# Attention, maxout and PReLU layers on one core: the last batch's gate stage, with its row splits, factor loads and weight loads put in another order

## The chip, the cores and the metric

The kernel runs on one core of one Trainium2 chip. The metric is the device time of one execution in microseconds (us), lower is better. Before the change it is 775.16 us, the median of three runs (775.11 to 776.03).

## What is computed

```python
def reference(q, k, v, ...):                      # 4 batches, 8 heads, 576 positions, 64 wide
    scores = q @ k.T / sqrt(64)                   # masked: 4 heads local, 4 heads strided
    x = softmax(scores) @ v                       # -> x: 2304 tokens x 512
    h = maximum(maximum(x @ w1, x @ w2), x @ w3)  # 512 -> 768, "gates"
    x2 = h @ w_out                                # 768 -> 512
    y = x2 @ w_in                                 # 512 -> 2048
    g = maximum(y, 0) + alpha * minimum(y, 0)
    return g @ w_out2                             # 2048 -> 512
```

All of it is in float32. The kernel splits each operand of a product into a high and a low part and makes three matmuls of them (high x high, high x low, low x high).

## The kernel before, in words

The program has two halves. In the first (to 413 us of the span), batches 0 to 2 go through attention, the three gate layers and the first output layer ("out1"), in an order made by a planner (`Weave`); the weights of the second layer pair are prepared meanwhile. The last batch's gates and out1 are written out by hand, as a generator, `last_net`. In the second half, three blocks of 768 tokens (each in two column halves of 384) go through the last two layers.

The change is in `last_net` and in the loop that drives it (`for n, _ in enumerate(last_net(B - 1))`). `last_net` yields after each unit of work, and the loop puts other work between units; n is the number of the unit.

- Units 0 to 11 (`GATES_LAST`) are ordinary gate products, 12 matmuls of 288 columns each (L570). Meanwhile eight factors of the tokens, "T1" to "T4", are made: `make(m)` splits them in high (ACT) and low (DVE).
- Units 12 to 53 are six groups of seven products (k = 3 to 8). A product is six matmuls into one of eight PSUM banks (L735). Seven products by Winograd's scheme give four quarters of one gate matrix times the tokens. Of each group ACT copies the first product out of its bank (L752), and DVE adds the six others up in a chain that starts from that copy (`add`, L722). A group belongs to g = 0, 1 or 2. With g = 1 and 2 DVE also takes the running maximum (`greatest`), and with g = 2 the finished h is split: ACT casts its high part, DVE makes its low part (L205, L208 in `split`). One factor pair ("ws", two tiles of 512 KB) is loaded for each group into the pool `hw` of eight tiles (`load_factors`).
- Units 54 to 61 are out1: eight products of 18 matmuls (L592), each copied out by ACT (L784) and stored to DRAM as x2.

Into these units the loop weaves the splitting of the second block's rows (block 1), which batches 1 and 2 have left in DRAM. For each of its two halves SP loads four row tiles ("xs", `early_load`), POOL makes four sums (`early_sums`, L805), and then seven `early_split`s follow, one every second unit: ACT casts the high part into a tile of pool `xst`, POOL makes the low part (L208), and one unit later SP stores the tile to DRAM ("xd<-xst", `early_store`, L829). The pool `xst` has two tiles, so a cast waits until the store of two splits earlier has landed. The loop also loads the nine first tiles of output weights ("w<-wo", `load_ow`, L855), one every four units from unit 12 on. Each engine works its instructions off in the order in which they are written, and SP issues all of the loads and stores in one queue.

Of the kernel before, what the change touches and what calls it, by code (L numbers as in the profile page):

```python
# [10 lines left out]
F32 = mybir.dt.float32  # L11
# [3 lines left out]
ALU = mybir.AluOpType  # L15
# [25 lines left out]
NOW = 9  # L41
NG = 3 * NF1 // 2
NP = 3
X_SPLIT = 13


class Weave:
# [112 lines left out]
def attention_maxout_prelu_kernel(  # L160
# [13 lines left out]
    nc = tc.nc  # L174
# [28 lines left out]
    def split(hi, lo, src, hi_engine, lo_engine):  # L203
        if hi_engine is nc.scalar:
            hi_engine.copy(hi, src)  # L205
        else:
            hi_engine.tensor_copy(hi, src)
        lo_engine.tensor_tensor(out=lo, in0=src, in1=hi.bitcast(F32), op=ALU.subtract)  # L208
# [5 lines left out]
    def pool(stack, name, bufs, side="left"):  # L214
        return stack.enter_context(tc.tile_pool(name=name, bufs=bufs, side=side, reuse_waits="tile"))
# [25 lines left out]
    def bank():  # L241
        return ps.tile([P, 512], F32, tag="bank", name="bank")
# [370 lines left out]
    GATES_LAST = [(hf, f) for f in range(2 * NP // 3) for hf in range(2)]  # L613
# [60 lines left out]
    def last_net(b):  # L674

        factors, st = {}, {}

        def load_factors(k):
            if k < NG:
                for i in range(2):  # L680
                    t = words["s", k, i] = hw.tile([P, 2, DM], F32R, tag="w", name="w")
                    nc.sync.dma_start(t.bitcast(F32), sd[k - NP][i][:, :, :])
            else:
                n, i = divmod(k - NG, 2)
                load_h(n, ((0, 2), (1, 3))[i])

        for k in range(NP, NP + 4):
            load_factors(k)
        rows = [[p_.tile([P, 2, HB], F32, tag=tag, name=tag) for _ in range(2)]
                for p_, tag in ((xsp, "xs"), (xst, "xst"))]  # L690
        for i in range(2):
            for r in range(2):
                for h in range(2):
                    x = xt[b, i + 2 * r, h].bitcast(F32)
                    nc.vector.tensor_tensor(out=rows[i][r][:, h, :HALF], in0=x[:, 0], in1=x[:, 1], op=ALU.add)
        named = []
        for i in range(2):
            b11, b12, b21, b22 = (t[:, h, :HALF] for t in rows[i] for h in range(2))
            t2, t3, t4 = (temp() for _ in range(3))
            for out_, x, y in ((t3, b22, b12), (b12, b12, b11), (t2, b22, b12), (t4, b21, t2)):  # L700
                nc.vector.tensor_tensor(out=out_, in0=x, in1=y, op=ALU.subtract)
            named += [("T1", i, b12), ("T2", i, t2), ("T3", i, t3), ("T4", i, t4)]
            for c, (name, h) in enumerate((("11", 0), ("21", 0), ("22", 1))):
                factors[name, i] = xt[b, i + 2 * (c > 0), h]
        named.sort(key=lambda it: it[0])

        def make(m):
            name, i, x = named[m]
            t = factors[name, i] = (xt[b, i, 1] if name == "T4" else
                                    (xp if m < 3 else tf).tile([P, 2, HALF], F32R, tag="x", name="x"))  # L710
            split(t[:, 0], t[:, 1], x, nc.scalar, nc.vector)

        for n, (hf, f, g) in enumerate(units(GATES_LAST)):
            gate_unit(b, hf, f, g, st)
            if n < 6:
                make(n)
            yield
        for m in range(6, 8):
            make(m)

        def add(out_, bank, other, op=ALU.add):
            nc.vector.tensor_tensor(out=out_, in0=bank, in1=other, op=op)  # L722

        for k in range(NP, NG):
            p, g = divmod(k, 3)
            w0, w1_ = (words["gate", 2 * p + j, g] for j in range(2))
            sa, sb = (words["s", k, i] for i in range(2))
            new = kept_temp if g == 0 else temp

            def product(w, off, name):  # L730
                bank_ = bank()[:, :HALF]
                m = 0
                for c in range(2):
                    for wi, xi in PAIRS:
                        nc.tensor.matmul(bank_, w[:, wi, off + c * P:off + (c + 1) * P],  # L735
                                         factors[name, c][:, xi, :], start=m == 0, stop=m == 5)
                        m += 1
                return bank_

            def greatest(hf, j, c):  # L740
                if g == 0:
                    st[hf, j] = c
                    return
                t = st[hf, j]
                add(t, t, c, ALU.max)
                if g == 2:
                    h = st["h", hf, 2 * p + j] = hp.tile([P, 2, HALF], F32R, tag="x", name="h")
                    split(h[:, 0], h[:, 1], t, nc.scalar, nc.vector)

            x = product(w0, 0, "11")  # L750
            u = new()
            nc.scalar.copy(u, x)  # L752
            yield
            x = product(sb, 256, "T2")
            v = new()
            add(v, x, u)
            yield
            x = product(w0, 256, "21")
            add(u, x, u)
            greatest(0, 0, u)  # L760
            yield
            x = product(sb, 0, "T3")
            w = new()
            add(w, x, v)
            yield
            x = product(w1_, 256, "T4")
            c21 = new()
            add(c21, x, w)
            greatest(0, 1, c21)
            yield  # L770
            x = product(sa, 0, "T1")
            add(w, x, w)
            add(v, x, v)
            greatest(1, 1, w)
            yield
            x = product(sa, 256, "22")
            load_factors(k + 4)
            add(v, x, v)
            greatest(1, 0, v)
            yield  # L780
        for hf in range(2):
            for dc in range(NCC):
                xo = tp.tile([P, HALF], F32, tag="t", name="xo")
                nc.scalar.copy(xo, out1_products(b, hf, dc, st))  # L784
                store_x2(b, hf, dc, xo)
                yield
# [23 lines left out]
    def split_x2(blk, k, i, pool, tag, lo_engine=nc.vector):  # L810

        t = pool.tile([P, 2, HB], F32R, tag=tag, name=tag)
        split(t[:, 0], t[:, 1], xs.pop((blk, PRODUCTS[k][1], i)), nc.scalar, lo_engine)
        return t

    early_rows, early_parts = {}, []

    def early_load(blk, i, pool, tag):
        early_rows[blk, i] = load_x2(blk, i, pool, tag)
# [1 line left out]
    def early_sums(blk, i):  # L821
        sum_x2(blk, i, early_rows.pop((blk, i)), nc.gpsimd)

    def early_split(blk, i, k):
        early_parts.append((blk, k, i, split_x2(blk, k, i, xst, "xst", nc.gpsimd)))

    def early_store():
        for blk, k, i, t in early_parts:
# [31 lines left out]
    for b in range(B):  # L860
        first, last = (-32, -8) if b == 0 else ((b - 1) * NUNITS + (16 if b == 1 else 3), b * NUNITS - 3)
# [24 lines left out]
    tsp = pool(ctx, "tsp", 3, "right")  # L886
    xst = pool(ctx, "xst", 2, "right")
    sx = ExitStack()
    tq = pool(sx, "tq", 8, "right")
    tf = pool(sx, "tf", 3, "right")  # L890

    def temp():
        return tq.tile([P, HALF], F32, tag="t", name="t")
# [1 line left out]
    def kept_temp():  # L895
        return tp.tile([P, HALF], F32, tag="t", name="t")

    ready = {X_SPLIT + 19 * half + 2 * k: (1, half, k) for half in range(2) for k in range(7)}
    first, gates = 3 * len(GATES_LAST), 3 * len(GATES_LAST) + 7 * (NG - NP)
    fetched = [first + 4 * i for i in range(9)]  # L900
    for n, _ in enumerate(last_net(B - 1)):
        if n in fetched:
            load_ow()
        if n - 1 in ready:
            early_store()
        for half in range(2):
            if n == X_SPLIT + 19 * half - 5 + 2 * half:
                early_load(1, half, xsp, "xs")
            if n == X_SPLIT + 19 * half - 1:
                early_sums(1, half)  # L910
        if n in ready:
            early_split(*ready[n])
        if n == gates - 5:
            rows = [load_x2(0, 0, xsp, "xs"), load_x2(0, 1, xst, "xst")]
        if n == gates - 1:
            sx.close()
            x0x.close()
            xmp = pool(ctx, "xmp", 1, "right")
        if n == gates:
            sum_x2(0, 0, rows[0], nc.vector)  # L920
        if n == gates + 1:
            sum_x2(0, 1, rows[1], nc.vector)
        for i, ks in {0: [(0, range(7))], 2: [(1, range(4))], 3: [(1, range(4, 7))]}.get(n - gates, []):
            for k in ks:
                x2h[0, k, i] = split_x2(0, k, i, xmp, f"x{k}{i}")
# [258 lines left out]
    for n in range(NQ * NBLK):  # L1184
        blk, q = divmod(n, NQ)
# [75 lines left out]
```

## Time and profile before

| | |
|---|---|
| median of three runs | 775.16 us |
| the profiled execution's own time | 777.17 us |
| its span, first to last instruction | 775.4 us |
| PE busy | 743.9 us, 96% of the span |
| DVE, ACT, POOL busy | 628.7, 466.0, 50.4 us |
| mean granted TensorE clock | 0.982 |
| matmuls of the gate groups (L735) | 252, 38.3 us busy, 9.1 us of idle time before them |

The page also cuts the span into 40 slices of 19.4 us. PE stands at 9 tenths in nearly all of them; apart from the start three neighbouring slices, the 19th to 21st, from about 349 to 407 us, are at 7, and in the last two of them the clock row stands at 8 tenths. The stretch of the last batch is there. Where rows below name a tile, "bank", "ph" and "po" are PSUM banks, "t" the temporary tiles, "xst" the split rows and "xd" their place in DRAM.

### The profile page before, as it was taken

Reading aid. Unit: us, or ns where it says so; the run is one execution under the profiler, and the core shown is the slowest. Engines: PE = TensorE matmul, PEld = TensorE weight load, DVE = VectorE, ACT = ScalarE, POOL = GpSimd, SP = SyncE. Lnnn points to the kernel's source line nnn. Section 1 sums busy time; section 2 is a strip of 40 time slices with the busy share of each in tenths; the row PEclk is TensorE's granted clock in tenths of the full one; section 3 lists DMA queues with packets and bytes.
Section 4 is the critical chain, followed back from the end, with each engine's and each line's share of the span. In section 5 each row is a group of like instructions: output and inputs, shape, how many; then the busy total and the mean of one; then the engine's idle time right before and its main releaser. Section 6 shows DMA issues by size and latency. Waiting matters only on the chain.

```text
span 775.4 us, 16198 instructions
## 1 busy us (share of the span) xinstructions
PE 743.9 (96%) x5668; PEld 724.1 (93%) x5668; DVE 628.7 (81%) x1663; ACT 466.0 (60%) x1252; POOL 50.4 (6%) x60
## 2 busy tenths in 40 slices
PE   5799999999999999997779999999999999999998
PEld 4699999999999999997779999999999999999997
DVE  4899998998998998555476988886988896888885
ACT  5987889568676896222135656654566554465571
POOL 1000000000000000032400211000211000000000
PEclk9789999999999999999889999999999999999999
DMA  6467769995999775669775889999888999877362
GB/s 239 144 222 238 225 209 328 354 358 204 331 334 337 259 252 213 240 244 339 247 268 174 265 266 315 353 400 376 299 316 289 344 403 375 278 253 251 122 186 87
DMA packets 88929, 211.97 MB, mean 273 GB/s; under 512 B 11024, under 2 KB 41232, under 8 KB 88848
## 3 DMA queue, kind: packets, MB, share of 16 engines
q1 hardware_dynamic: 88848, 210.94, 78.4%
q8 instruction: 45, 0.74, 0.4%
q14 instruction: 36, 0.29, 0.1%
HBM read 154.80 MB, written 56.10 MB: 272 GB/s over the span
## 4 chain that ended last, share of the span: by engine, by line
PE 80%; DMA 8%; DVE 5%; ACT 2%; POOL 2%; issue 1%; SPq 1%; DVEq 0%; ACTq 0%; POOLq 0%
PE ph L1122 21%; PE bank L570 21%; PE po L954 18%; PE bank L592 9%; PE ph L954 3%; DMA xd<-xst 3%; PE bank L311 3%; PE bank L382 3%; PE bank L357 2%; DMA w<-ws 1%; POOL xst L208 1%; DMA xs<-x 1%; DMA w<-wo 1%; DMA wo<-w 1%; DVE e L319 1%
## 5 line engine op out<-in xcount | busy, mean ns | idle before, releaser
L1122 PE MATMUL ph<-x,w 128*128 128x384 f32 x990 | 199.9, 337 | 0.6 <-ACT c L1132 0.5
L570 PE MATMUL bank<-x,w 128*128 128x288 f32 x1440 | 197.9, 297 | 0.0
L570 PEld LDWEIGHTS bank<-x,w 128*128 128x128 f32 x1440 | 192.5, 189 | 1.9 <-issue 0.2
L954 PE MATMUL po<-w,g 128*128 128x256 f32 x1296 | 181.1, 281 | 0.0
L954 PEld LDWEIGHTS po<-w,g 128*128 128x128 f32 x1296 | 174.9, 189 | 0.3
L1122 PEld LDWEIGHTS ph<-x,w 128*128 128x128 f32 x990 | 165.2, 188 | 1.0 <-ACT c L1132 0.7
L1128 DVE TENSOR_TENSOR c<-ph,c 128x384 f32<-128x384 f32 x165 | 89.2, 553 | 39.2 <-PE ph L1122 38.2
L947 ACT CAST g<-c 128x384 fp32r<-128x384 f32 x96 | 48.6, 506 | 90.4 <-DVE c L1106 48.9
L592 PE MATMUL bank<-h,w 128*128 128x288 f32 x576 | 82.5, 302 | 5.0 <-ACT h L205 4.9
L592 PEld LDWEIGHTS bank<-h,w 128*128 128x128 f32 x576 | 79.0, 193 | 7.0 <-ACT h L205 5.5
L326 ACT ACTIVATE e<-e,nm 96x128 f32<-96x128 f32 (+2 forms) x176 | 68.0, 395 | 7.6 <-DVE nm L319 7.6
L250 ACT CAST w<-word 128x512 fp32r<-128x512 f32 x100 | 57.5, 587 | 22.6 <-DMA wh<-w 8.4
L253 DVE TENSOR_TENSOR w<-word,w 128x512 fp32r<-128x512 f32 x100 | 62.8, 641 | 9.4 <-ACT w L250 9.1
L1072 ACT ACTIVATE c<-c 128x384 f32<-128x384 f32 x96 | 50.5, 526 | 32.2 <-DVE c L1128 30.9
L1076 DVE SCALAR_TENSOR_TENSOR c<-c 128x384 f32<-128x384 f32 x96 | 54.7, 570 | 8.7 <-ACT c L1073 8.7
L1073 ACT ACTIVATE c<-c,nalpha 128x384 f32<-128x384 f32 x96 | 59.2, 617 | 3.1
L948 DVE TENSOR_TENSOR g<-c,g 128x384 fp32r<-128x384 f32 x96 | 55.1, 573 | 1.9 <-ACT g L947 1.9
L441 ACT ACTIVATE word<-raw 128x512 f32<-128x512 f32 x56 | 37.5, 676 | 18.3 <-DMA raw<-in_w 14.7
L735 PE MATMUL bank<-x,w 128*128 128x288 f32 x252 | 38.3, 313 | 9.1 <-ACT t L752 6.9
L735 PEld LDWEIGHTS bank<-x,w 128*128 128x128 f32 x252 | 36.5, 203 | 10.8 <-ACT t L752 7.6
L948 DVE TENSOR_TENSOR g<-k,g 128x384 fp32r<-128x384 f32 x72 | 36.9, 550 | 8.0 <-ACT g L947 8.0
L1106 DVE TENSOR_TENSOR k<-c 128x384 f32<-128x384 f32 x72 | 40.3, 587 | 0.0
(93 smaller groups left out, 834.0 us busy)
## 6 DMA issues: line engine op xcount, KB each, us to landing
w<-wh SPq DMA_DIRECT2D x72, 512.0 KB, 5.5
raw<-in_w SPq DMA_DIRECT2D x50, 512.0 KB, 4.7
w<-wo SPq DMA_DIRECT2D x48, 512.0 KB, 6.1
w<-wp SPq DMA_DIRECT2D x36, 512.0 KB, 7.0
wh<-w SPq DMA_DIRECT2D x24, 512.0 KB, 5.1
xd<-xst SPq DMA_DIRECT2D x28, 384.0 KB, 6.0
x<-xd SPq DMA_DIRECT2D x28, 384.0 KB, 8.4
ws<-w SPq DMA_DIRECT2D x12, 512.0 KB, 3.9
```

The source lines that it names most:

```text
L250: (nc.scalar.copy if e == "ACT" else nc.vector.tensor_copy)(out_, in_)
L253: nc.vector.tensor_tensor(out=out_, in0=x, in1=y, op=ALU.subtract)
L326: nc.scalar.activation(tl[ek][:nq, j, i, :nk], tl[ek][:nq, j, i, :nk], AF.Exp, bias=tl["nm", u][:nq, j, i:i + 1], scale=-1.0, accum_out=tl ...
L570: nc.tensor.matmul(acc, words["gate", f, g][:, wi, cc * P:(cc + 1) * P], xt[b, cc, hf][:, xi, :], start=n == 0, stop=n == 3 * NCC - 1)
L592: nc.tensor.matmul(acc, words["mix", f][:, wi, dc * P:(dc + 1) * P], st["h", hf, f][:, xi, :], start=n == 0, stop=n == 3 * NF1 - 1)
L735: nc.tensor.matmul(bank_, w[:, wi, off + c * P:off + (c + 1) * P], factors[name, c][:, xi, :], start=m == 0, stop=m == 5)
L948: return g, lambda: nc.vector.tensor_tensor(out=g[:, 1], in0=x, in1=g[:, 0].bitcast(F32), op=ALU.subtract)
L954: nc.tensor.matmul(bank[:, NH * half:NH * (half + 1)], g[:, gi, t * P:(t + 1) * P], w[:, wi, off:off + NH], start=first and i == 0, stop=l ...
L1073: nc.scalar.activation(a, a, AF.Copy, scale=nalpha[:, f:f + 1])
L1076: nc.vector.scalar_tensor_tensor(out=a, in0=h, scalar=0.0, in1=a, op0=ALU.max, op1=ALU.add)
L1122: nc.tensor.matmul(bank, words["h", n, i][:, wi, off + c * P:off + (c + 1) * P], x2h[blk, k, c][:, xi, :], start=m == 0, stop=m == 5)
L1128: nc.vector.tensor_tensor(out=out_, in0=bank, in1=other, op=ALU.add)
```

## The change

- `X_SPLIT` goes from 13 to 10: the first half's splits stand three units earlier. The second half's stay at units 32 to 44 (10 + 22 instead of 13 + 19).
- `early_load` of the two halves moves from units 8 and 29 to 2 and 23, `early_sums` from 12 and 31 to 8 and 30.
- A second pool of two tiles, `xsu`, takes every other split, so a cast waits for the store of four splits earlier. To make room `tq`, which holds the temporaries, goes from eight tiles to six.
- The first four factor pairs are no longer loaded in one go, but one at the start and the others after units 3, 5 and 7, with the row loads between the first two.
- The nine loads of output weights move from units 12 to 44 to units 53 to 61, behind the gates.
- The low part of an h is recorded in a list and issued by `make_lows` after the matmuls of the next product.

```diff
-X_SPLIT = 13
+X_SPLIT = 10
...
-        for k in range(NP, NP + 4):
-            load_factors(k)
+        load_factors(NP)
...
             if n < 6:
                 make(n)
+            if n in (3, 5, 7):
+                load_factors(NP + n // 2)
             yield
...
+        lows = []
+
+        def make_lows():
+            while lows:
+                h, t = lows.pop(0)
+                nc.vector.tensor_tensor(out=h[:, 1], in0=t, in1=h[:, 0].bitcast(F32), op=ALU.subtract)
...
+                make_lows()
                 return bank_
...
-                    split(h[:, 0], h[:, 1], t, nc.scalar, nc.vector)
+                    nc.scalar.copy(h[:, 0], t)
+                    lows.append((h, t))
...
+            if k == NG - 1:
+                make_lows()
             yield
...
-    def early_split(blk, i, k):
-        early_parts.append((blk, k, i, split_x2(blk, k, i, xst, "xst", nc.gpsimd)))
+    def early_split(blk, i, k, pool=None):
+        early_parts.append((blk, k, i, split_x2(blk, k, i, pool or xst, "xst", nc.gpsimd)))
...
-    tq = pool(sx, "tq", 8, "right")
+    tq = pool(sx, "tq", 6, "right")
     tf = pool(sx, "tf", 3, "right")
+    xsu = pool(sx, "xsu", 2, "right")
...
-    ready = {X_SPLIT + 19 * half + 2 * k: (1, half, k) for half in range(2) for k in range(7)}
-    first, gates = 3 * len(GATES_LAST), 3 * len(GATES_LAST) + 7 * (NG - NP)
-    fetched = [first + 4 * i for i in range(9)]
+    ready = {X_SPLIT + 22 * half + 2 * k: (1, half, k) for half in range(2) for k in range(7)}
+    gates = 3 * len(GATES_LAST) + 7 * (NG - NP)
+    fetched = [gates - 1 + i for i in range(9)]
...
-            if n == X_SPLIT + 19 * half - 5 + 2 * half:
+            if n == X_SPLIT + 21 * half - 8:
                 early_load(1, half, xsp, "xs")
-            if n == X_SPLIT + 19 * half - 1:
+            if n == X_SPLIT + 22 * half - 2:
                 early_sums(1, half)
         if n in ready:
-            early_split(*ready[n])
+            early_split(*ready[n], (xst, xsu)[n // 2 % 2])
```

The order on SP from the second half's row loads to its fourth store, before. "xs<-x" are the row loads, "wh" the first tiles of the next layer's weights, "wo" the output weights, "ws" the factors, "xd_k_h" the store of split k of half h:

```order
L829 DMA xd_6_0_133<-xst 128x768
L855 DMA w<-wo_0_109 128x1024
L797 DMA xs<-x_2_69 128x384
L797 DMA xs<-x_3_70 128x384
L843 DMA w<-wh_0_73 128x1024
L843 DMA w<-wh_2_75 128x1024
L855 DMA w<-wo_1_110 128x1024
L829 DMA xd_0_1_122<-xst 128x768
L829 DMA xd_1_1_124<-xst 128x768
L855 DMA w<-wo_0_111 128x1024
L829 DMA xd_2_1_126<-xst 128x768
```

And with the change:

```order
L841 DMA xd_6_0_133<-xst 128x768
L809 DMA xs<-x_2_69 128x384
L809 DMA xs<-x_3_70 128x384
L682 DMA w<-ws_0_159 128x1024
L682 DMA w<-ws_1_160 128x1024
L855 DMA w<-wh_0_73 128x1024
L855 DMA w<-wh_2_75 128x1024
L841 DMA xd_0_1_122<-xst 128x768
L841 DMA xd_1_1_124<-xst 128x768
L841 DMA xd_2_1_126<-xst 128x768
```

(The four row loads stand as two pairs of such lines.) The output weights are gone from between the stores, and the row loads now stand ahead of the last factor pair.

On ACT, the casts of the first half's splits and the copies that start a group, as the difference of the two programs stands there: before,

```order
L752 COPY t<-bank 128x288
L205 CAST xst<-xs 128x384
L205 CAST xst<-t 128x384
L205 CAST xst<-xs 128x384
L752 COPY t<-bank 128x288
L205 CAST xst<-t 128x384
L205 CAST xst<-xs 128x384
L205 CAST xst<-t 128x384
L205 CAST xst<-xs 128x384
L752 COPY t<-bank 128x288
```

and with the change (ahead of these rows one cast stands before the last gate units' cast of h):

```order
L762 COPY t<-bank 128x288
L205 CAST xst<-t 128x384
L205 CAST xst<-xs 128x384
L205 CAST xst<-t 128x384
L205 CAST xst<-xs 128x384
L762 COPY t<-bank 128x288
L205 CAST xst<-t 128x384
L205 CAST xst<-xs 128x384
L762 COPY t<-bank 128x288
```

Four casts stood ahead of the third group's copy, and now two do. In the second half ACT's order is the same in both programs.

On DVE, the first low parts of the last group (g = 2): before,

```order
L722 TENSOR_TENSOR t<-bank,t 128x288 x2
L722 TENSOR_TENSOR t<-t 128x288
L208 TENSOR_TENSOR h<-t,h 128x288
L722 TENSOR_TENSOR t<-bank,t 128x288 x2
L722 TENSOR_TENSOR t<-t 128x288
L208 TENSOR_TENSOR h<-t,h 128x288
```

and with the change:

```order
L723 TENSOR_TENSOR t<-bank,t 128x288 x2
L723 TENSOR_TENSOR t<-t 128x288
L730 TENSOR_TENSOR h<-t,h 128x288
L723 TENSOR_TENSOR t<-bank,t 128x288 x2
L723 TENSOR_TENSOR t<-t 128x288
L730 TENSOR_TENSOR h<-t,h 128x288
```

Only the line numbers differ: each low part (`h<-t,h`) still stands right behind its maximum (`t<-t`).

## Rows read from the trace of the kernel before

**Rows 1.** Busy time by stretch: width, engines' busy us, granted clock, DMA share, GB/s.

```profile
319.50:338.50 19.00, 19.00 (x146) 19.00 (x145) 9.59 (x23) 5.30 (x14) 1.37 (x2) 1.00 0.79 300
338.50:374.00 35.50, 30.62 (x218) 28.93 (x216) 21.05 (x44) 8.54 (x20) 15.54 (x16) 1.00 0.72 263
374.00:396.00 22.00, 12.85 (x59) 11.84 (x60) 10.00 (x23) 4.45 (x10) 5.64 (x6) 0.73 0.85 282
396.00:413.00 17.00, 17.00 (x123) 17.00 (x123) 12.68 (x27) 8.61 (x22) 0.00 (x0) 0.94 0.59 200
```

**Rows 2.** Timeline of PE: start, length, line, matmuls, idle time before and what ended it.

```profile
305.14 14.55 PE L592 MATMUL bank<-h,w 128*128 128x288 f32 x108
...
338.56 3.91 PE L735 MATMUL bank<-x,w 128*128 128x288 f32 x28
343.00 14.15 PE L735 MATMUL bank<-x,w 128*128 128x288 f32 x104 [0.52 <-DVE x L208]
...
378.23 7.77 PE L735 MATMUL bank<-x,w 128*128 128x288 f32 x36 [4.58 <-ACT t L752]
...
391.49 1.34 PE L592 MATMUL bank<-h,w 128*128 128x288 f32 x3 [3.88 <-ACT h L205]
...
413.04 2.24 PE L1122 MATMUL ph<-x,w 128*128 128x384 f32 x12
```

**Rows 3.** Waits, 330 to 410 us: who waited for whom, us, times, longest.

```profile
ACT xst L205 <- DMA xd<-xst: 27.1, 10, 5.0
```

**Rows 4.** Timeline of ACT around the last group's start.

```profile
380.98 0.52 ACT L205 CAST xst<-xs 128x384 fp32r<-128x384 f32 x1 [2.80 <-DMA xd<-xst]
386.46 0.51 ACT L205 CAST xst<-t 128x384 fp32r<-128x384 f32 x1 [4.96 <-DMA xd<-xst]
...
389.04 0.39 ACT L752 COPY t<-bank 128x288 f32<-128x288 f32 x1
```

**Rows 5.** Landing times, from the views of the stores (first) and of the row loads.

```profile
DMA to landing us min/median/max: 2.3/3.9/6.7
DMA to landing us min/median/max: 5.7/7.2/9.9
```

**Rows 6.** Timeline of POOL: one low part, and the second half's first sum.

```profile
357.62 1.01 POOL L208 TENSOR_TENSOR xst<-xs,xst 128x384 fp32r<-128x384 f32 x1 [1.67 <-ACT xst L205]
368.44 1.02 POOL L805 TENSOR_TENSOR t<-xs 128x384 f32<-128x384 f32 x1 [9.80 <-DMA xs<-x]
```

**Rows 7.** Timeline of DVE: two factors, then groups with g = 0, 2 and 1.

```profile
340.49 2.45 DVE L208 TENSOR_TENSOR x<-t,x 128x288 fp32r<-128x288 f32 x2
342.87 3.42 DVE L722 TENSOR_TENSOR t<-bank,t 128x288 f32<-128x288 f32 x7
...
349.64 0.89 DVE L722 TENSOR_TENSOR t<-t 128x288 f32<-128x288 f32 x1
...
357.88 1.02 DVE L722 TENSOR_TENSOR t<-bank,t 128x288 f32<-128x288 f32 x2 [5.39 <-ACT t L752]
...
362.27 0.46 DVE L208 TENSOR_TENSOR h<-t,h 128x288 fp32r<-128x288 f32 x1 [0.50 <-ACT h L205]
...
366.15 0.46 DVE L208 TENSOR_TENSOR h<-t,h 128x288 fp32r<-128x288 f32 x1 [0.50 <-ACT h L205]
...
378.21 1.02 DVE L722 TENSOR_TENSOR t<-bank,t 128x288 f32<-128x288 f32 x2 [7.01 <-ACT t L752]
...
383.30 0.46 DVE L722 TENSOR_TENSOR t<-t 128x288 f32<-128x288 f32 x1
```

**Rows 8.** Timeline of DVE: block 0's rows, from the first sum to the last low part.

```profile
399.07 0.56 DVE L805 TENSOR_TENSOR t<-xs 128x384 f32<-128x384 f32 x1 [0.89 <-DMA xs<-x]
...
409.78 0.55 DVE L208 TENSOR_TENSOR x<-xst,x 128x384 fp32r<-128x384 f32 x1
```

**Rows 9.** Timeline of SP: issues of the second half's row loads.

```profile
359.52 3.12 SPq L797 DMA_DIRECT2D xs<-x  x4
```

**Rows 10.** Timeline of PE: the first matmuls that use output weights.

```profile
421.36 0.51 PE L954 MATMUL po<-w,g 128*128 128x256 f32 x3
```

## The prediction

> **What bounds the kernel now.** I read the slices of the page first: PE is full except in the last batch's stretch. The view by stretch makes that exact [rows 1]: PE is busy without a gap until 338.5 us, then idle for 35.50 - 30.62 = 4.9 us up to 374 and for 22.00 - 12.85 = 9.2 us up to 396, and full again after that. The granted clock, 1.00 before, is 0.73 in the second of these stretches, a mix of the two levels (1.2 and 2.4 GHz) that follows PE's idle time.
>
> What would the stage take without that? PE's timeline [rows 2] gives undisturbed rates: 104 gate matmuls in 14.15 us are 0.136 us each, 108 out1 matmuls in 14.55 us are 0.1347 each. So 252 gate matmuls need 34.3 us and 144 out1 matmuls 19.4, together 53.7. They take from 338.56 to 413.04, where the next layer's first product begins: 74.5 us. There are **20.8 us** to be had, 14.0 of them idle time and the rest matmuls at a lower clock (36 in 7.77 us are 0.216 each).
>
> Who holds PE? The same timeline names ACT's copy of a group's first product before the largest gap (4.58 us), and ACT's cast of h before the next (3.88). On ACT these two are late because of the split casts written ahead of them: ACT waited 27.1 us in ten waits for stores of split rows [rows 3]. The clearest place is the last group [rows 4]: casts start at 380.98, 386.46 and just before 389.04, each after a wait for a store, and only then runs the copy, 0.39 us long. PE had been some seven products ahead, filled all eight banks, and stopped. A store takes 2.3 to 6.7 us to land [rows 5], and with two tiles every cast waits for the store of two splits earlier. A second cause is the row loads of the second half: POOL's first sum waited 9.80 us for them [rows 6], and everything behind it shifted.
>
> **The change, part by part.**
>
> *Four tiles.* A cast waits for the store of four splits earlier. A round trip is the cast (0.51), POOL's low part (1.01 [rows 6]), some 0.5 for hand-overs and issue, and the store: 5.9 us at the median landing, 8.7 at the longest. Per split that is 1.5 and 2.2 us instead of 3.0 and 4.4. Splits are written one per two products, 1.63 us. So the median store now just keeps up, and a group holds at most four casts.
>
> *First half.* Its loads and sums move ahead by six and four units, its splits by three, and no weights stand between its stores. The first cast runs ahead of the last h cast of the gate units, at about 336; three follow the first group's copy at about 340.5 without a store to wait for; the fifth needs the first store (issued about 338). POOL ends its seventh low part near 348.5. The second and third copies, due at about 345.5 and 351, are not held. Gain: the waits ahead of them go.
>
> *Second half.* Its casts keep their units (32 to 44); only loads, sums and tiles differ. The loads can be issued when the first half's seventh low part is done, 348.5, and take 3.12 us to issue [rows 9]. With landings of 7.2 us (median) they are there by 356 to 358. Four sums at 1.02 bring POOL to 361.5, and low parts follow every 1.0 us. The first store then lands at about 362.5 + 0.3 + 3.9 = 366.7, so the fifth, sixth and seventh casts run at about 367, 368 and 369, and the last group's copy at 369.3. The product that it copies is ready at 338.56 + 0.5 + 35 products of 0.817 + 0.8 = 368.5. It is 0.8 us late, and PE has seven more banks, 5.7 us: no stop. With the longest landings (9.9 and 6.7 us) it is 6.3 us late; that is a rival.
>
> *DVE, which is next in line.* A group with g = 0 takes it 3.42 us, with g = 1 5.55 (378.21 to 383.76), with g = 2 8.73 (357.88 to 366.61) [rows 7]. Six groups are 35.4 us against PE's 34.3: it nearly keeps pace. From the end of the first group's adds (346.3) the others end at 351.9, 360.6, 364.1, 369.6 and 378.3. PE leaves the last group at about 373.4, and no bank is asked for before it is read. out1's first product asks for the second h's low part after 16 of its matmuls, at 375.5; DVE has it 4.85 us into the group (362.27 + 0.46 - 357.88), at 374.5. So there is about 1 us to spare, and I charge 0.3 us, between 0 and the 4 us of the rival below.
>
> *Low parts a product later: nothing.* DVE's order of instructions is the same before and after. The low part still stands directly behind the maximum, so the 0.50 us that it waits for ACT's cast [rows 7] stays, four times in each group with g = 2. They are in the 8.73.
>
> *Temporaries 8 to 6.* Each tile is asked for again only after six others; what it held was last read a group earlier on DVE itself. Cost 0; it is hidden by DVE's own order.
>
> *Factors in turn.* The second pair is now behind the rows on SP, but is needed only at the second group, at 345; SP issued eight such loads in 4 us, and the DMA share is 0.79 there [rows 1]. Cost 0.
>
> *The factor T4.* PE waited 0.52 us for it [rows 2], as DVE took 2.45 us for two splits while POOL was summing [rows 7]. POOL's sums are now earlier but its low parts are there; I leave the 0.5 us in.
>
> *Weights behind the gates.* Nine loads of 512 KB move from the stage to out1. First use is 8.3 us after 413.04 [rows 2, 10], so at about 401 now, and the first of them is issued at about 373. Block 0's rows stand ahead of them. DVE needs 11.3 us for these rows [rows 8]; from 378.3 it ends at 389.6, and PE is ready at 393. Cost 0.
>
> **Sum.** 20.8 - 0.5 - 0.3 = 20.0 us. The profiled execution took 777.17, so it would take 757.2; the median is 2.0 us below the profiled one, and 20.0 off 775.16 gives **755.2**.
>
> **Rivals.**
>
> *The casts still wait* (0.12). If the row loads or stores land as late as the slowest seen, the last group's copy is 6.3 us late. The second h's low part then comes at about 374.8 + 0.4 + 4.85 = 380 for a demand at 375.5: 4.5 us lost, 759.7; if PE's clock falls over it (36 matmuls at 0.216 instead of 0.136), 2.9 more, 762.6. For it: the second half's casts have not moved. Against: less is moved in the stage.
>
> *DVE takes over, through POOL* (0.08). Operations with two tiles in SBUF are slow beside POOL: 2.45 us for two instead of 0.92, 0.89 for a maximum instead of 0.46 [rows 7], while adds out of a bank stay at 0.46. Such losses come to some 3 us in the stage, and the sum keeps them. Twice as many put DVE's end at 381 and PE some 2.5 us back: 757.7. If each of POOL's 22 operations held up one of the 26 such DVE operations for its whole 1.0 us, DVE would be 22 - 3 = 19 us later and nothing gained: 774. The Trainium skill, "SBUF — State Buffer", section "SBUF: two separate sides", states that the two engines share one pair of ports as an exclusive lock, so that the loser blocks for the whole instruction; by that rule packing POOL's work closer works against this change, by between 0 and those 19 us. The trace agrees with the rule's direction (0.89 instead of 0.46), and no run here shows yet how often they meet.
>
> *The weights come too late, and it is slower* (0.03). In out1 SP must now move nine weight tiles, block 0's rows (1.57 MB), two more tiles of 0.79 MB and x2 (1.18 MB), 8.3 MB in all, from 373. At 282 GB/s that is 29 us, to 402; at the 200 of the last stretch [rows 1] 41 us, to 414. If the output products had to wait for all nine, the first would lose 13 us at 200 GB/s (768), and below 170 GB/s, 49 us, more than 20: slower than before. At 160 it would be 779. Against: only the first tile is needed first, and the stretches with loads waiting moved 263 to 300.
>
> *No difference* (0.02): what ends the waits is something that the trace does not name.
>
> **How the numbers follow.** The forecast (0.75) reaches from 753.0 (nothing left over, and half a us for the runs' spread) to 757.5. The range takes in DVE's near case and the first of the late landings: 753.0 to 760.0; outside are the deeper cases of the three rivals, about 0.13. What a measurement of this kernel can tell from no change is about 0.2%, 1.6 us. Faster by more than that are the forecast and nearly all of the first two rivals: 0.94. Within it are the "no difference" case and DVE's far end: 0.03. Slower: 0.03.
>
> **What would show it.** Right: the 252 gate matmuls end at about 373 and the next layer's first product begins at 392.5 to 393.5; the granted clock stays near 1.00 in between; ACT's waits for stores fall from 27.1 to under 8 us; PE names ACT's copy for under 1 us; the low parts' waits of 0.50 are still there. Wrong: a gap on PE of over 2 us with ACT's copy behind it (the casts), DVE's groups longer than 3.4, 5.6 and 8.7 us with PE waiting for banks (POOL), or PE waiting for a weight load after 400.

## The result, and the profile after

The changed kernel takes 755.45 us (median of five runs, 753.71 to 757.36), the kernel before beside it 775.68 us (five runs, 775.11 to 777.19). The ratio is 0.9737, with a 95% interval of 0.9715 to 0.976: 20.2 us faster, where 20.0 were forecast.

The profiled execution took 753.71 us, with a span of 751.9. The view by stretch of the changed kernel (width, busy us of PE, PEld, DVE, ACT and POOL, granted clock, DMA share, GB/s) answers to [rows 1]:

```profile
338.50:374.00 35.50, 34.42 (x256) 33.98 (x255) 28.28 (x61) 8.74 (x21) 15.84 (x16) 1.00 0.89 319
374.00:392.00 18.00, 18.00 (x132) 18.00 (x131) 12.68 (x27) 9.49 (x24) 0.00 (x0) 1.00 0.93 306
```

Idle time of PE falls from 14.0 to 1.1 us, and the clock stays at its upper level. The DMA engines, which were busy for 0.72 and 0.85 of the time and moved 263 and 282 GB/s, now are for 0.89 and 0.93 and move 319 and 306. PE's timeline, beside [rows 2]:

```profile
334.54 33.77 PE L743 MATMUL bank<-x,w 128*128 128x288 f32 x252
368.15 2.18 PE L592 MATMUL bank<-h,w 128*128 128x288 f32 x15
371.31 17.71 PE L592 MATMUL bank<-h,w 128*128 128x288 f32 x129 [0.99 <-ACT h L757]
388.87 2.27 PE L1135 MATMUL ph<-x,w 128*128 128x384 f32 x12
```

All 252 gate matmuls run as one piece, and one gap of 0.99 us is left in out1. In the following, "the stage" is the time from the first gate group's matmul to the next layer's first product, read off such rows. It was 413.04 - 338.56 = 74.5 us and is now 388.87 - 334.54 = 54.3.

The waits in the changed kernel, beside [rows 3] (who waited for whom, us, times, longest):

```profile
ACT xst L205 <- DMA xd<-xst: 4.1, 3, 2.8
DVE h L730 <- ACT h L757: 4.0, 8, 0.5
```

ACT's waits for stores fall from 27.1 to 4.1 us. The eight waits of 0.50 us of DVE's low parts are all there. ACT's timeline in the second half, beside [rows 4]:

```profile
358.71 0.40 ACT L762 COPY t<-bank 128x288 f32<-128x288 f32 x1
361.88 0.51 ACT L205 CAST xst<-xs 128x384 fp32r<-128x384 f32 x1 [2.77 <-DMA xd<-xst]
362.87 0.52 ACT L205 CAST xst<-t 128x384 fp32r<-128x384 f32 x1 [0.47 <-DMA xd<-xst]
364.20 0.52 ACT L205 CAST xst<-xs 128x384 fp32r<-128x384 f32 x1 [0.82 <-DMA xd<-xst]
364.62 0.39 ACT L762 COPY t<-bank 128x288 f32<-128x288 f32 x1
```

The casts still wait, but for 4.1 us in all, and the last group's copy runs 30.1 us into the stage instead of 50.5.

The spans differ by 23.5 us, not 20.2. Of that the stage gives 20.15. It also begins 4.0 us earlier, and what follows it is 0.7 us longer (363.0 instead of 362.4). The earlier start is not the change's doing: the last batch's first gate unit already starts at 315.50 instead of 319.52, and in the kernel with casts on POOL below, which is the kernel before up to that unit, it starts at 316.00. The last section comes back to this.

### The profile page after: what moved, and what is told of

Same layout as the page of the kernel before. It is cut to its first block, busy times and chain, and to the rows that moved or that the text cites. A ratio compares the mean times of both kernels' runs of the same rounds, so it can differ in the third digit from the quotient of the medians.

```text
span 751.9 us, 16191 instructions
## 1 busy us (share of the span) xinstructions
PE 732.7 (97%) x5668; PEld 715.3 (95%) x5668; DVE 630.8 (84%) x1663; ACT 464.4 (62%) x1252; POOL 50.2 (7%) x60
## 4 chain that ended last, share of the span: by engine, by line
PE 91%; DVE 5%; ACT 3%; issue 1%; DMA 0%; DVEq 0%; SPq 0%; ACTq 0%
PE bank L570 26%; PE ph L1135 22%; PE po L967 19%; PE bank L592 10%; PE ph L967 3%; PE bank L311 3%; PE bank L382 3%; PE bank L357 2%; PE bank L743 2%; DVE t L723 2%; ACT e L326 1%; DVE g L961 1%; DVE e L319 0%; DMA k<-in_kTs 0%; DVE k L1119 0%
## 5 line engine op out<-in xcount | busy, mean ns | idle before, releaser
L570 PE MATMUL bank<-x,w 128*128 128x288 f32 x1440 | 197.2, 296 | 0.0
L570 PEld LDWEIGHTS bank<-x,w 128*128 128x128 f32 x1440 | 191.8, 188 | 1.8
L592 PE MATMUL bank<-h,w 128*128 128x288 f32 x576 | 79.9, 297 | 1.1 <-ACT h L757 1.0
L592 PEld LDWEIGHTS bank<-h,w 128*128 128x128 f32 x576 | 77.0, 188 | 2.4 <-ACT h L757 1.2
L250 ACT CAST w<-word 128x512 fp32r<-128x512 f32 x100 | 57.4, 588 | 28.4 <-DMA wh<-w 8.8
L1085 ACT ACTIVATE c<-c 128x384 f32<-128x384 f32 x96 | 50.5, 526 | 32.4 <-DVE c L1141 31.0
L447 DVE SCALAR_TENSOR_TENSOR word<-raw,word 128x512 uint32<-128x512 uint32 x56 | 38.8, 693 | 1.9
L960 ACT CAST g<-k 128x384 fp32r<-128x384 f32 x72 | 33.4, 514 | 7.9 <-PE ph L967 4.0
```

What stands on the lines that cost most here:

```text
L250: (nc.scalar.copy if e == "ACT" else nc.vector.tensor_copy)(out_, in_)
L570: nc.tensor.matmul(acc, words["gate", f, g][:, wi, cc * P:(cc + 1) * P], xt[b, cc, hf][:, xi, :], start=n == 0, stop=n == 3 * NCC - 1)
L592: nc.tensor.matmul(acc, words["mix", f][:, wi, dc * P:(dc + 1) * P], st["h", hf, f][:, xi, :], start=n == 0, stop=n == 3 * NF1 - 1)
L960: nc.scalar.copy(g[:, 0], x)
```

## The experiments

The change has three parts that can stand alone: **tiles** (four tiles, six temporaries), **weights** (output weights behind the gates) and **rows** (order of row loads, factors and first splits). The first four kernels take them one at a time, or leave the tiles out. Each was profiled, and timed beside the kernel before. That took 777.29 us beside these four and 777.23 beside the next ones, some 2 us more than the 775.16 from which my expectations start, so a miss of 2 us in a time says little; the ratio and the stage say more. The six temporaries always come with the four tiles: no run takes them alone.

**Tiles alone.**

```diff
-    tq = pool(sx, "tq", 8, "right")
+    tq = pool(sx, "tq", 6, "right")
+    xsu = pool(sx, "xsu", 2, "right")
...
-            early_split(*ready[n])
+            early_split(*ready[n], (xst, xsu)[ready[n][2] % 2])
```

> The kernel before with one part of the change alone: four tiles for the split rows (and six temporaries instead of eight). Theory A (ACT stands still because a cast waits for the store of two splits earlier; the number of tiles is the cause): the first half's casts run free, the second half's still start late, since its row loads stay at unit 29 with weights in front of them (rows there at about 362 instead of 354, the last group's copy some 6 us late, 4 to 5 us lost on PE). So 760 us, between 758 and 763; ACT's waits for stores fall from 27 to under 12 us. Theory B (the order of the transfers is the cause: row loads come late and 512 KB weight loads stand between the stores; tiles matter little): 768 or more.

Measured: 767.57 us, ratio 0.9892 (0.9864 to 0.9921); stage 402.95 - 336.59 = 66.4 us. That fits neither theory: ACT's waits fell to 13.0 us in five, near what theory A asked for, yet the gain was 8 us instead of 15. The landing times of the stores of split rows, in the kernel with tiles alone, point to the reason:

```profile
DMA to landing us min/median/max: 2.3/7.7/9.5
```

They landed after 7.7 us at the median, against 3.9 before [rows 5]. With four tiles the stores follow each other faster, and the 512 KB loads between them are still there. PE still stopped for 3.20 us behind the copy and for 2.23 and 1.35 us in out1. The table below, where each part is there and is not, bears the reading out.

**Weights alone, rows alone, and both without tiles** (the last is the changed kernel with all splits in one pool).

```diff
-    fetched = [first + 4 * i for i in range(9)]
+    fetched = [gates - 1 + i for i in range(9)]
```

> The kernel before with the nine output weight loads moved behind the gates, and nothing else. Theory A: stores land sooner (about 3 us instead of 3.9), but with two tiles a pair of casts still takes a round trip of about 5 us against 3.3 us of products, so ACT's waits stay above 15 us: 765 to 770. Theory B: the stores and row loads are the cause, so most of the gain is here: 762 or less.

```diff
-X_SPLIT = 13
+X_SPLIT = 10
...
-        for k in range(NP, NP + 4):
-            load_factors(k)
+        load_factors(NP)
...
+            if n in (3, 5, 7):
+                load_factors(NP + n // 2)
...
-            if n == X_SPLIT + 19 * half - 5 + 2 * half:
+            if n == X_SPLIT + 21 * half - 8:
...
-            if n == X_SPLIT + 19 * half - 1:
+            if n == X_SPLIT + 22 * half - 2:
```

> The kernel before with the loads in another order and the first half's splits three units earlier (rows ahead of the later factors, second half's rows six units earlier), with two tiles and the weights in their old place. Theory A: two tiles and weights between the stores keep ACT waiting, more than 18 us: 766 to 771. Theory B: 762 or less.

```diff
-            early_split(*ready[n], (xst, xsu)[n // 2 % 2])
+            early_split(*ready[n])
```

> The changed kernel with all splits in the two tiles of the first pool again; all else as changed. Theory A: casts wait for the store of two splits earlier again; in the second half the copies of the last two groups are each some 8 us late, of which PE's banks hide 5.7: 8 to 10 us lost, 763 to 766. Theory B: 758 or less.

Measured: weights 771.51 us, ratio 0.9919 (0.9888 to 0.995), stage 409.52 - 338.65 = 70.9; rows 772.31 us, ratio 0.9958 (0.9937 to 0.9979), stage 409.53 - 336.39 = 73.1; both 767.66 us, ratio 0.9894 (0.986 to 0.9927), stage 402.67 - 336.24 = 66.4. ACT waited 24.9, 28.6 and 20.8 us for stores. Theory B is out: without the four tiles nothing comes near 762. Theory A had the direction. By the ratios the gains are 6.3, 3.3 and 8.2 us, where it put at least 5.2, 4.2 and 9.2 (and at least 12.2 for tiles alone, which gave 8.4): weights alone did a little better than its least, the three others worse. This led to a new theory C, that the causes need each other.

**Two parts at a time.** Tiles and weights is the kernel before with the two edits above; tiles and rows is the changed kernel with the weights back:

```diff
-    fetched = [gates - 1 + i for i in range(9)]
+    fetched = [first + 4 * i for i in range(9)]
```

> The kernel before with four tiles and with the output weights behind the gates, but the row loads, factors and first splits in their old order. New theory C (two causes that need each other: four tiles let casts go on only if no weight loads stand between the stores; with them the stores land after 7.7 us instead of 3.9, as the kernel with tiles alone showed): most of the 20 us is here; the rows of the second half come some 4 us later than in the changed kernel, which the banks hide: the stage from the first gate group's product to the next layer's first is 55 to 58 us (54.3 in the changed kernel, 74.5 before, 66.4 with tiles alone), the time 755 to 759. If the order of rows and factors is the missing part instead: stage over 61 us, time over 762.

> The changed kernel with the nine output weight loads back in the gate units. Theory C: the stores wait behind weight loads again (landing about 7 us at the median), so ACT's waits for stores rise from 4 us to 10 or more and the stage from 54.3 to 60 to 65 us: 760 to 766. If the order of rows and factors is what tiles alone lacked: stage under 57 us, under 758.

Measured: tiles and weights 761.87 us, ratio 0.9799 (0.9784 to 0.9814), stage 396.86 - 339.12 = 57.7; tiles and rows 761.1 us, ratio 0.979 (0.9773 to 0.9806), stage 395.58 - 336.51 = 59.1. The stage of the first lies where theory C put it, at its upper end, the time 3 us above, of which 2 are the slower kernel before. The second came out 1 us better on the stage than expected, and within the range on the time (by the ratio 1 us better there too); ACT waited 7.4 us for stores, not 10 or more. With that all eight combinations have a trace. The last two columns count from the start of the stage: the start of POOL's first sum of the second half's rows, and the end of POOL's low part in the last split. For that the lines of the kernel before and of the changed kernel are:

```profile
389.21 0.99 POOL L208 TENSOR_TENSOR xst<-xs,xst 128x384 fp32r<-128x384 f32 x1 [1.17 <-ACT xst L205]
```

```profile
364.80 1.02 POOL L208 TENSOR_TENSOR xst<-xs,xst 128x384 fp32r<-128x384 f32 x1 [0.28 <-ACT xst L205]
```

| parts | stage, us | stores land, median us | ACT waits for stores, us | second half's sums begin, us | last split done, us |
|---|---|---|---|---|---|
| none | 74.5 | 3.9 | 27.1 | 29.9 | 51.6 |
| rows | 73.1 | 2.9 | 28.6 | 26.3 | 49.6 |
| weights | 70.9 | 3.2 | 24.9 | 27.6 | 47.1 |
| weights, rows | 66.4 | 2.7 | 20.8 | 23.2 | 42.6 |
| tiles | 66.4 | 7.7 | 13.0 | 28.7 | 42.7 |
| tiles, weights | 57.7 | 4.5 | 4.6 | 22.8 | 35.0 |
| tiles, rows | 59.1 | 6.4 | 7.4 | 21.1 | 36.1 |
| all (the change) | 54.3 | 4.4 | 4.1 | 19.3 | 31.3 |

The gains of the single parts, 1.3, 3.6 and 8.1 us, add up to 13.1; together they give 20.2. Each part is worth most behind the other two: the tiles 12.1 us (66.4 to 54.3), the weights 4.8 and the rows 3.4. The last column goes with the stage: in all eight kernels the stage ends 22.8 to 23.9 us after the last split is done. The third column shows one way in which the parts meet: more tiles let more stores out at once, which costs landing time (3.9 to 7.7), and taking the weights away gives it back (7.7 to 4.5).

**Is ACT's queue the way by which late stores stop PE?** Here the casts of the second block's splits go to POOL, in the kernel before, with its two tiles and its order of loads.

```diff
-        early_parts.append((blk, k, i, split_x2(blk, k, i, xst, "xst", nc.gpsimd)))
+        early_parts.append((blk, k, i, split_x2(blk, k, i, xst, "xst", nc.gpsimd,
+                                                nc.gpsimd if blk == 1 else nc.scalar)))
```

> The kernel before with the second block's split casts on POOL instead of ACT (POOL does cast and low part of each split); tiles, loads and weights as before. If ACT's queue is the way by which late stores stop PE: ACT never waits for a store, the gate groups and out1 run with no gap over 0.6 us (252 gate matmuls in about 34.5 us, out1 in 19 to 20), although the stores still take as long. The chain of splits itself does not get shorter, rather longer (two POOL operations of about 1 us for each, two tiles), so it comes out elsewhere: block 0's rows wait for the last splits, and PE stands before the next layer's first product, 8 to 18 us. Stage 62 to 72 us, time 763 to 772. If PE was held by the transfers or by DVE and not by ACT's queue: gaps of several us remain inside the gate groups.

Measured: 777.45 us, ratio 1.0026 (1.0002 to 1.0049); stage 408.86 - 335.04 = 73.8. PE's timeline of this kernel:

```profile
335.04 23.48 PE L735 MATMUL bank<-x,w 128*128 128x288 f32 x174
358.73 10.62 PE L735 MATMUL bank<-x,w 128*128 128x288 f32 x78 [0.20 <-ACT t L752]
369.19 2.21 PE L592 MATMUL bank<-h,w 128*128 128x288 f32 x15
373.09 0.40 PE L592 MATMUL bank<-h,w 128*128 128x288 f32 x1 [1.69 <-ACT h L205]
374.38 18.76 PE L592 MATMUL bank<-h,w 128*128 128x288 f32 x128 [0.89 <-DVE h L208]
408.86 4.21 PE L1123 MATMUL ph<-x,w 128*128 128x384 f32 x12 [15.72 <-ACT xo L784]
```

The gate groups run through: 34.2 us for 252 matmuls, with one gap of 0.20 us. So inside the groups it was ACT's queue through which PE was held, as the prediction said. In out1 2.6 us of gaps remained, which I had not expected; DVE was slower with more of POOL's work beside it (one low part of an h took 1.25 us instead of 0.46). And nothing is gained: PE stands for 15.72 us before the next layer instead. The profile names ACT's xo copy; behind it, on the chain of waits of the same kernel (start, us, what), stand these links:

```profile
381.20 5.47 DMA xd<-xst
...
387.31 1.02 POOL xst L208
...
389.24 6.48 DMA w<-wh
...
395.74 2.83 DMA xst<-x
...
398.57 0.57 DVE xs L805
```

The last split is done at 388.3, SP issues block 0's row loads after it, the last of them on this chain behind a weight load, and DVE sums and splits what they bring. My range was wrong: the stage is 1.8 us beyond it and the time 5 us, because I let the chain end too early; the gap of 15.72 us lay within the 8 to 18 expected. The chain of rows, splits and stores thus sets the stage either way, here through block 0's rows and in the kernel before through ACT's queue. The same view of the kernel before says so too: from 341 to 389 us its chain runs over POOL, the split casts, these stores and the row loads, and only at the end over ACT's copy:

```profile
382.61 5.92 DMA xd<-xst
...
388.62 0.51 ACT xst L205
389.13 0.31 ACT t L752
```

The last split is done 53.3 us into the stage with the casts on POOL and 51.6 before. How long the chain would be with neither ACT's late casts nor POOL's added work is not shown.

**The low parts.** First comes the changed kernel with the split in one place again, as before the change; then with the low part truly later in DVE's order, behind the next product's adds.

```diff
-                    nc.scalar.copy(h[:, 0], t)
-                    lows.append((h, t))
+                    split(h[:, 0], h[:, 1], t, nc.scalar, nc.vector)
```

```diff
-                make_lows()
                 return bank_
...
             add(w, x, v)
+            make_lows()
             yield
```

(Likewise after the first product's copy and after the adds of the sixth and seventh products, ahead of `greatest`.)

> The changed kernel with each h split in one place again, as before the change. DVE's and ACT's instructions stand in the same order either way, so nothing changes: same time within 0.3%, stage 54.0 to 54.7 us, eight waits of 0.50 us for ACT's cast on DVE, 1.0 us of wait on PE. If the list of low parts did matter: over 757 and a longer stage.

> The changed kernel with each low part issued on DVE behind the next product's adds, so that it truly stands later in DVE's order. The cast is done by then: the eight waits of 0.50 us fall to under 1 us in total, a group with g = 2 takes DVE some 7 us instead of 8.7, PE's wait of 0.99 us in the first out1 product goes, and the stage is 53.2 to 53.6 us. Time 0.5 to 1.5 us below the changed kernel, which the timed runs may not tell apart. If DVE's lag does not set PE's wait: stage 54.3 still.

Measured: with the split in one place 754.74 us, ratio 0.9708 (0.968 to 0.9736), stage 389.01 - 335.60 = 53.4; with low parts behind the adds 755.13 us, ratio 0.9708 (0.9682 to 0.9734), stage 389.82 - 337.13 = 52.7. The times of the two and of the changed kernel (0.9737, 0.9715 to 0.976) cannot be told apart. The split in one place was 0.6 us below my expectation of the stage: PE's wait of 0.99 us was not in that execution. Its longest wait of ACT for a store was 1.8 us, in the changed kernel's 2.8, with the same order on DVE. So I took the changed kernel and the last one again:

> The changed kernel once more, unchanged, for a second trace of it. If PE's wait of 0.99 us in out1 belongs to that one execution (a store that landed late): a stage of 53.3 to 54.4 us, the wait between 0 and 1 us, going with the longest of ACT's waits for a store. If it belongs to the kernel: 54.3 us and 1.0 us again.

> The kernel with the low parts truly later on DVE once more, unchanged. Stage 52.6 to 53.0 us, no wait of PE for the cast of h, whatever the stores do.

The changed kernel, once more: stage 392.18 - 337.83 = 54.35, PE's wait 1.05 us, ACT's longest wait 2.8. The other: 396.44 - 343.75 = 52.7, no such wait. The wait came back and so did the late store, so this alone does not tell my two explanations apart. DVE's trace says more. PE waits there for the cast of the second h of the last group, and the cast for DVE, which from the start of the fourth group to that cast stands still only for its own low part's 0.50 us: no store and no copy holds it. What differs is one maximum beside a low part of POOL's. In the changed kernel POOL's starts first and DVE's takes 1.20 us (again in its second execution):

```profile
363.50 1.01 POOL L208 TENSOR_TENSOR xst<-t,xst 128x384 fp32r<-128x384 f32 x1
363.63 1.20 DVE L723 TENSOR_TENSOR t<-t 128x288 f32<-128x288 f32 x1
```

With the split in one place the same maximum starts first, and it is POOL's next low part that takes longer than its usual 1.01 us:

```profile
364.65 0.46 DVE L723 TENSOR_TENSOR t<-t 128x288 f32<-128x288 f32 x1
364.68 1.30 POOL L208 TENSOR_TENSOR xst<-xs,xst 128x384 fp32r<-128x384 f32 x1
```

These 0.74 us are most of the 0.9 by which DVE begins the last group later in the changed kernel. The late store goes with POOL's low parts standing later (that of the sixth split 1.2 us later into the stage), but that it alone makes the two meet was not tested.

DVE's timeline in the last group, with low parts behind adds (first execution), beside [rows 7]:

```profile
368.18 1.01 DVE L723 TENSOR_TENSOR t<-bank,t 128x288 f32<-128x288 f32 x2
...
370.19 0.46 DVE L730 TENSOR_TENSOR h<-t,h 128x288 fp32r<-128x288 f32 x1
...
374.81 0.46 DVE L730 TENSOR_TENSOR h<-t,h 128x288 fp32r<-128x288 f32 x1 [0.50 <-ACT h L756]
```

The group takes 7.1 us (368.18 to 375.27) instead of 8.73, and only its last low part still waits. PE's timeline of the same execution has no gap:

```profile
337.13 33.77 PE L743 MATMUL bank<-x,w 128*128 128x288 f32 x252
370.74 19.24 PE L592 MATMUL bank<-h,w 128*128 128x288 f32 x144
389.82 2.25 PE L1138 MATMUL ph<-x,w 128*128 128x384 f32 x12
```

In both of its executions the stage is 52.7 us, 0.5 below the range that I gave and 1.6 under the changed kernel's: it is the shortest stage here, though the times do not resolve it. In its second execution the maximum beside POOL took 1.20 us as well, and PE did not wait.

## Why the prediction was right, point by point

- *The time to be had.* 53.7 us of matmuls at undisturbed rates were 1.0 too many: with the low parts behind the adds, and no gap, the stage took 52.7, of them 33.6 for the gate groups (34.3 assumed) and 19.1 for out1 (19.4). So 21.8 us were to be had and not 20.8. The changed kernel's stage is 54.3, a gain of 20.2 for 20.0 forecast.
- *Four tiles, second half.* The fifth to seventh casts were put 28.4 to 30.4 us into the stage and the last copy at 30.7, 0.8 us late; they ran at 27.3 to 29.7 and 30.1. The rows landed after 6.4 us at the median for 7.2.
- *What was left over.* I charged 0.5 us for the factor T4 and 0.3 for DVE's lag, 0.8 in all; the changed kernel takes 1.6 above the 52.7. The first charge was gone: the two splits took 0.82 us instead of 2.45, and POOL was idle then. The second was 0.99, or 0 with the split in one place. The rest, some 0.6, lies in out1, in no wait of 0.2 us or more that the profile names on PE. That the sum came out within 0.2 us is luck: 1.0 too little to be had and 0.8 too little left over cancel.
- *DVE next in line.* From the first group's start DVE's last low part ends at 375.63 - 334.54 = 41.1 us; forecast was 378.3 - 338.56 = 39.7. It is late by 1.4, and PE came to out1 1.2 us sooner than forecast. The 1 us to spare was too little for that, and PE met DVE at the second h.
- *Low parts: nothing.* Shown: the same waits of 0.50 us, eight of them, and the same time without the edit.
- *Behind the gates.* Output weights never stopped PE. The cover for block 0's rows was thinner than said: DVE finished its last low part at 388.48, PE began the next layer at 388.87, where I had 3 us to spare. Part of it is DVE's wait of 1.59 us for the row loads. With tiles and weights alone PE did wait there, 1.40 us for an xo copy.
- *The rival of POOL and DVE* did not come at its price. From the last h of the gate units on, 27 operations of DVE with two tiles in SBUF took 15.4 us before and 15.1 now; at the 0.456 us of an undisturbed one they would be 12.3, so the loss was 3.1 us and is 2.8. But it is not nothing: one such meeting is 0.74 of the 0.99 us that PE still waits. The lock that the Trainium skill ("SBUF — State Buffer", "SBUF: two separate sides") describes shows in its direction, with maxima of up to 1.20 us, but far from the 22 us of a full block by each of POOL's operations. The lines of the changed kernel, by form, for the 16 maxima and the 8 low parts (busy us, mean ns, idle before):

```profile
L723 DVE TENSOR_TENSOR t<-t 128x288 f32<-128x288 f32 x16 | 9.4, 590 | 0.4
L730 DVE TENSOR_TENSOR h<-t,h 128x288 fp32r<-128x288 f32 x8 | 4.4, 551 | 4.0 <-ACT h L757 4.0
```

- *The step that was too simple* is the one on who holds PE. It put PE's stops down to the split casts in ACT's queue and the stores that they wait for. The kernel with casts on POOL showed that the queue was only the way: take it away, and the chain of loads, splits and stores holds PE at another place, with a stage of 73.8 us instead of 74.5. The forecast still held, because the three parts of the change together shorten that chain: the last split is done 31.3 us into the stage instead of 51.6, 20.3 us sooner, and the stage is 20.2 shorter. By the prediction's account the tiles alone should have given most of it (theory A put 15 us on them), and they gave 8.

## What to carry to other kernels

When an engine stalls behind a wait in its queue, follow that wait's own chain to its end before pricing its removal: moving the casts to another engine took the stall out of the groups and won nothing. Deeper buffers ahead of a store need room in the queue too; here four tiles alone doubled the stores' landing time, and paid in full only once the loads that were not yet needed had been moved behind. And code moved in the source has moved only if the engine's own order of instructions has.

## What the hardware showed beyond that

The part of the program ahead of the stage took between 334.5 and 343.8 us in these executions, though PE's instructions there are the same in all. The two ends, by stretch from 20 to 40 us, are the changed kernel and the second execution with low parts behind adds:

```profile
20.00:40.00 20.00, 16.19 (x181) 13.01 (x180) 18.12 (x101) 19.85 (x85) 0.00 (x0) 0.91 0.51 172
```

```profile
20.00:40.00 20.00, 15.49 (x161) 12.08 (x163) 17.20 (x95) 19.21 (x82) 0.00 (x0) 0.83 0.48 155
```

In the kernel before the clock of that stretch was 0.73. PE is idle for some 4 us of it in each, and the clock then stands for a different part of it at the lower of its two levels. The clock of this stretch does not order the executions by itself: the one at 343.8 also lost time at 150 to 250 us, where PE was busy for 95.8 of 100 us; why is open. For a change of 20 us in one stage this does not matter, but a difference of one or two us is better read from the stage's own rows than from the time.
